# The low part of w2's rows on GpSimd in the one-block dense layers of a linear-attention kernel

## The chip, the cores and the metric

The kernel runs on one core of a Trainium2 chip. The metric is the device time of one execution in microseconds. TensorE (PE) multiplies matrices, VectorE (DVE), ScalarE (ACT) and GpSimd (POOL) work elementwise, and SyncE (SP) issues nearly all transfers. Each engine runs its own queue in order and waits on semaphores for the others.

## What is computed

Two rounds of a linear-attention layer A and a dense layer B on x of 2048 x 576, all in float32:

```python
def _A_ref(x, wqkv, w_phi, wo):          # H = 32 heads of 18
    q, k, v = heads(x @ wqkv)
    pq, pk = q @ w_phi, k @ w_phi         # per head
    phi_q = concat(softmax(pq), softmax(-pq))
    phi_k = concat(softmax(pk), softmax(-pk))
    kv, z = phi_k.T @ v, phi_k.sum(over s)
    return (phi_q @ kv / (phi_q @ z + 1e-6)) @ wo

def _B_ref(x, w1, b1, w2, b2):           # 576 -> 4608 -> 576
    h = relu(x @ w1 + b1)
    return (h * h) @ w2 + b2

x = A_x
for _ in range(2):
    x = x + _A_ref(layernorm(x), A_wqkv, A_w_phi, A_wo)
    x = x + _B_ref(layernorm(x), B_w1, B_b1, B_w2, B_b2)
```

## The kernel before

The 2048 rows are four blocks of 512. A matrix product in float32 is made of three products of parts: each operand is split into a high part, which ScalarE writes in the type fp32r that TensorE multiplies, and a low part, the operand less its high part, which VectorE or GpSimd subtracts. High x high, high x low and low x high are summed.

Each round has, behind a barrier at which the sums over all keys are complete, a dense layer for each block. Two blocks are done one by one with `g_mlp` (a first pass and a second pass), the other two together with `g_pair`. In the trace the first pass of the first round is `m_3`, the second pass `m_2`, and in the second round `m_1` and `m_0`; they lie at about 219 to 498, 490 to 808, 1426 to 1705 and 1694 to 2017 us, and both rounds run nearly alike. Beside the first pass runs the attention of the next block (`back_first`), beside the second pass that of the last two (`back_second`): tiles named `a_0`, `a_1`, `a_2`, `a_3`. The function `weave` interleaves the two by a rate, and `chained` keeps the steps of the attention in their order on VectorE, ScalarE and GpSimd. The final order of each engine's queue is set when the program is built, by a planner with costs and due times, so it can differ from the order in which the lines are traced; `tc.issue_after` fixes one instruction behind another.

A pass goes over 36 groups f of 128 hidden features. For each group:

- `first(f)` loads w1's columns into r1 (L1159, L244) and w2's rows into r2 (L1161). ScalarE makes the high parts: L1167 of w1, L1168 of the 448 columns of w2 that `by_rows` uses, L1169 of the 128 that `features` uses. The low part of w1 is L1171. `low()` makes the two low parts of w2: L1174 for the rows (128x448, VectorE), L1175 for the features (128x128, GpSimd).
- `hidden(f)` is 14 matmuls on x (L1190), `square(f)` applies bias, Relu and Square on ScalarE (L1197 to L1199) and makes the low part of the result on VectorE (L1200).
- `second(f - 1)` is 12 matmuls by rows (L1217) and 3 for the features (L1208). The high part of w2 enters in the first matmul of L1217, the low part in the second.

r1, r2, h1 and s2 have two buffers each, so r2 is loaded for a group when both low parts of the group two before are done.

For the first pass of a round `g_mlp` is called with `rest`, the unfinished end of the attention behind the keys. Then the first two groups are `early`: L1171 is on GpSimd for them, and `low()` is called later, behind given instructions. In all other groups `early` is false.

The attention that runs beside has its own work on the same queues: VectorE and GpSimd share products and scalings (L652 and L653, L835, L853), VectorE sums (L661, L841) and transposes the features (L897), SyncE stores them (L900) and loads them back turned (L928), ScalarE and VectorE split them (L941, L942), TensorE multiplies (L964, L999), and GpSimd adds b2 (L1051). At the end of the second pass the first operands of `g_pair` are prepared (L1478 to L1487 on GpSimd).

Of the kernel before, what the change touches and what calls it, by code (L numbers as in the profile page):

```python
# [7 lines left out]
F32 = mybir.dt.float32  # L8
# [13 lines left out]
def layers_kernel(  # L22
# [18 lines left out]
    nc = tc.nc  # L41
# [26 lines left out]
    RO = 16  # L68
# [25 lines left out]
    def wtile(name):  # L94
        n = len(spare["tags"])
        spare["i"] += 1
        i = spare["i"] % (n + 2)
        if i < n:
            return ps_a.tile([P, TB], F32, tag=spare["tags"][i], name=name)
        return ps_w.tile([P, TB], F32, tag="w", name=name)  # L100
# [140 lines left out]
    def load_twice(dst, src, c0, n):  # L241

        for i in range(2):
            nc.sync.dma_start(dst[i * DT : (i + 1) * DT], src[KC * P :, c0 : c0 + n])  # L244
# [902 lines left out]
    def g_mlp(layer, b, x, after, name, rest=None, then=None):  # L1147
# [3 lines left out]
        R = D - P  # L1151
# [3 lines left out]
        def first(f, early=False):  # L1155
            cols = slice(f * P, (f + 1) * P)
            r1 = sb.tile([P, NC, P], F32, tag="r1", name=f"{name}r1_{f}")
            r2 = sb.tile([P, D], F32, tag="r2", name=f"{name}r2_{f}")
            nc.sync.dma_start(r1[:, :KC], w1[: KC * P, cols].rearrange("(c p) n -> p c n", p=P))  # L1159
            load_twice(r1[:, KC], w1, f * P, P)  # L1160
            nc.sync.dma_start(r2, w2[cols])  # L1161
            hl1 = sb.tile([P, NC * HP], F32R, tag="h1", name=f"{name}h1_{f}")
            h1 = hl1[:, : NC * P].rearrange("p (c n) -> p c n", n=P)
            l1 = hl1[:, NC * P : 2 * NC * P].rearrange("p (c n) -> p c n", n=P)
            s2 = sb.tile([P, NC * HP], F32R, tag="s2", name=f"{name}s2_{f}")
            with tc.issue_after(dense["turn", 2 * f + 1].ins) if early else nullcontext():
                nc.scalar.activation(h1, r1, AF.Copy)  # L1167
            nc.scalar.activation(s2[:, RO : RO + R], r2[:, :R], AF.Copy)  # L1168
            nc.scalar.activation(s2[:, FC : FC + P], r2[:, R:], AF.Copy)  # L1169
            with tc.issue_after(dense["scaled1"].ins) if early else nullcontext():  # L1170
                dense["lowered"] = (nc.gpsimd if early else nc.vector).tensor_sub(l1, r1, h1.bitcast(F32))  # L1171

            def low():
                nc.vector.tensor_sub(s2[:, RO + R : RO + 2 * R], r2[:, :R], s2[:, RO : RO + R].bitcast(F32))  # L1174
                nc.gpsimd.tensor_sub(s2[:, FC + P : FC + 2 * P], r2[:, R:], s2[:, FC : FC + P].bitcast(F32))  # L1175

            if early:
                lows.append(low)
            else:
                low()  # L1180
            ph = wtile(f"{name}ph{f}") if f == 1 else ps_a.tile([P, TB], F32, tag="h", name=f"{name}ph{f}")
            parts[f] = (h1, l1, s2, ph)
# [650 lines left out]
    for layer in range(2):  # L1833
        ready, raws = barrier(layer, b, prev, x, xprev, kes, vpair, qpair)
        spare["tags"] = []
        early, operands, rows, nxt, keep = [], {}, [], {}, {}
# [148 lines left out]
```

## Time and profile before

| | |
|---|---|
| median of 3 runs | 2440.04 us (2438.57 to 2442.45) |
| the profiled execution | 2441.59 us |
| its span, first to last instruction | 2439.9 us |
| mean granted TensorE clock | 0.998 |
| PE busy | 2410.0 us (99%) |
| DVE busy | 1560.5 us (64%) |
| ACT busy | 1289.7 us (53%) |
| POOL busy | 940.6 us (39%) |

The columns of a row of the trace in order of time: start in us, duration in us, engine, line of the kernel, operation, output tile <- input tiles, shapes, count, and in brackets how long the engine sat idle before and what ended that. Rows of like instructions in a stretch are merged, with their count. In the view by groups stand the busy time and the mean in ns, and then the idle time before the group with what ended it. In the view of waits stand the waiting line, what it waited for, the total in us, how often, and the longest. In the view by stage each engine's busy time stands with its number of instructions, and then the granted clock and the transfers. A queue of an engine's sequencer has a q behind its name (SPq).

### The profile page before, as it was taken

What the parts mean: (1) busy time and instruction counts of PE and PEld (TensorE: products, weight loads), DVE (VectorE), ACT (ScalarE), POOL (GpSimd) and SP (SyncE); (2) the same over time, 40 slices, a digit from 0 to 9 for tenths busy, and PEclk for the clock granted to TensorE, in tenths of its full rate; (3) what the DMA queues carried; (4) which work ended last, traced back from release to release, by engine and by line L of the source; (5) the groups of instructions that cost most, each with busy time, mean ns of one, the idle gap of its engine ahead of it and who ended that gap; (6) DMA issues with size and microseconds to landing.
All of it is one profiled execution on the core that took longest, in us unless ns stands there. A gap on an engine that the chain in (4) does not pass through costs nothing. (4 is left out here: it accounts for less than half of the span.)

```text
span 2439.9 us, 41475 instructions
## 1 busy us (share of the span) xinstructions
PE 2410.0 (99%) x14806; PEld 2137.9 (88%) x14806; DVE 1560.5 (64%) x2537; ACT 1289.7 (53%) x2543; POOL 940.6 (39%) x1121
## 2 busy tenths in 40 slices
PE   9999999999999999999999999999999999999999
PEld 8999888888888888888999988888887888888898
DVE  8779847664867655545766787486557675555443
ACT  4344555444456666664443444554455466676643
POOL 4555303212335565542433442032222455565321
PEclk9999999999999999999999999999999999999999
DMA  9124573666654533338753156537667444333364
GB/s 338 64 84 165 163 194 97 151 202 220 155 173 136 157 99 115 109 104 302 257 188 139 59 173 143 168 96 186 191 233 158 141 142 145 118 103 116 110 199 130
DMA packets 370646, 379.40 MB, mean 155 GB/s; under 512 B 142886, under 2 KB 270790, under 8 KB 367878
## 3 DMA queue, kind: packets, MB, share of 16 engines
q1 hardware_dynamic: 369180, 375.37, 51.2%
q8 instruction: 116, 1.90, 0.3%
q10 hardware_dynamic: 1258, 1.37, 0.2%
q14 instruction: 92, 0.75, 0.1%
HBM read 297.22 MB, written 79.41 MB: 154 GB/s over the span
## 5 line engine op out<-in xcount | busy, mean ns | idle before, releaser
L1507 POOL TENSOR_TENSOR m_ps<-m_pr,m_ps 128x128 fp32r<-128x128 f32 x144 | 98.6, 685 | 337.8 <-ACT m_ps L1505 310.7
L1506 DVE TENSOR_TENSOR m_ps<-m_pr,m_ps 128x448 fp32r<-128x448 f32 x144 | 99.8, 693 | 175.9 <-ACT m_ps L1504 175.8
L1549 PE MATMUL m_pacc<-m_ps,m_phb 128*128 128x448 f32 x864 | 185.6, 363 | 0.0
L1549 PEld LDWEIGHTS m_pacc<-m_ps,m_phb 128*128 128x128 f32 x864 | 161.9, 188 | 15.0
L1549 PE MATMUL m_pacacc<-m_ps,m_phc 128*128 128x448 f32 x648 | 147.1, 365 | 0.0
L1504 ACT ACTIVATE m_ps<-m_pr 128x448 fp32r<-128x448 f32 x144 | 82.8, 575 | 115.7 <-issue 64.9
L1549 PEld LDWEIGHTS m_pacacc<-m_ps,m_phc 128*128 128x128 f32 x648 | 119.2, 188 | 7.7
L1190 PE MATMUL m_0ph<-a_0nh,m_0h 128*128 128x512 f32 (+1 forms) x380 | 96.7, 382 | 1.6 <-ACT m_0hr L1197 1.4
L1190 PE MATMUL m_1ph<-t1onh,m_1h 128*128 128x512 f32 (+1 forms) x380 | 96.2, 381 | 2.0 <-ACT m_1hr L1197 1.8
L1217 PE MATMUL m_2acc<-m_2s,m_2hb 128*128 128x448 f32 x432 | 95.2, 367 | 2.9 <-ACT m_2s L1168 2.6
L1190 PE MATMUL m_3ph<-t0onh,m_3h 128*128 128x512 f32 (+1 forms) x380 | 96.1, 381 | 1.8 <-ACT m_3hr L1197 1.6
L1217 PE MATMUL m_0acc<-m_0s,m_0hb 128*128 128x448 f32 x432 | 95.0, 367 | 2.9 <-ACT m_0s L1168 2.6
L1190 PE MATMUL m_2ph<-a_2nh,m_2h 128*128 128x512 f32 (+1 forms) x380 | 96.6, 382 | 0.8 <-ACT m_2hr L1197 0.6
L1217 PE MATMUL m_3acc<-m_3s,m_3hb 128*128 128x448 f32 x432 | 94.2, 364 | 2.0 <-ACT m_3hb L1198 1.4
L1217 PE MATMUL m_1acc<-m_1s,m_1hb 128*128 128x448 f32 x432 | 94.2, 364 | 2.0 <-ACT m_1hb L1198 1.4
L1217 PEld LDWEIGHTS m_2acc<-m_2s,m_2hb 128*128 128x128 f32 x432 | 81.8, 190 | 11.7 <-ACT m_2s L1168 3.0
L1217 PEld LDWEIGHTS m_0acc<-m_0s,m_0hb 128*128 128x128 f32 x432 | 81.5, 190 | 11.7 <-ACT m_0s L1168 3.0
L1217 PEld LDWEIGHTS m_3acc<-m_3s,m_3hb 128*128 128x128 f32 x432 | 80.4, 188 | 10.6 <-ACT m_3hb L1198 2.1
L1217 PEld LDWEIGHTS m_1acc<-m_1s,m_1hb 128*128 128x128 f32 x432 | 80.4, 188 | 10.5 <-ACT m_1hb L1198 2.1
L1175 POOL TENSOR_TENSOR m_3s<-m_3r,m_3s 128x128 fp32r<-128x128 f32 x36 | 22.9, 637 | 161.9 <-ACT m_3s L1169 153.3
L1175 POOL TENSOR_TENSOR m_1s<-m_1r,m_1s 128x128 fp32r<-128x128 f32 x36 | 22.8, 635 | 162.0 <-ACT m_1s L1169 151.8
L1190 PEld LDWEIGHTS m_1ph<-t1onh,m_1h 128*128 128x128 f32 x380 | 68.8, 188 | 17.4 <-ACT m_1hr L1197 3.0
(2464 smaller groups left out, 7237.0 us busy)
## 6 DMA issues: line engine op xcount, KB each, us to landing
m_pr<-in_B_w SPq DMA_DIRECT2D x144, 288.0 KB
m_pr<-in_B_w SPq DMA_DIRECT2D x72, 256.0 KB
hd<-m_pu SPq DMA_DIRECT2D x72, 256.0 KB
m_pg<-hd SPq DMA_DIRECT2D x72, 256.0 KB
m_3r<-in_B_w SPq DMA_DIRECT2D x36, 288.0 KB
m_2r<-in_B_w SPq DMA_DIRECT2D x36, 288.0 KB
m_1r<-in_B_w SPq DMA_DIRECT2D x36, 288.0 KB
m_0r<-in_B_w SPq DMA_DIRECT2D x36, 288.0 KB
```

Source lines behind the costliest of these rows:

```text
L1175: nc.gpsimd.tensor_sub(s2[:, FC + P : FC + 2 * P], r2[:, R:], s2[:, FC : FC + P].bitcast(F32))
L1190: dense["hidden"] = nc.tensor.matmul(ph[:, cols], a, m, start=(k == 0), stop=(k == len(ops) - 1))
L1217: nc.tensor.matmul(acc[t][:, :R], a[:, rows], m, start=(f == 0 and k == 0), stop=(f == NF - 1 and k == 2))
L1504: nc.scalar.activation(s2[:, RO : RO + R], r2[:, :R], AF.Copy)
L1506: nc.vector.tensor_sub(s2[:, RO + R : RO + 2 * R], r2[:, :R], s2[:, RO : RO + R].bitcast(F32))
L1507: nc.gpsimd.tensor_sub(s2[:, FC + P : FC + 2 * P], r2[:, R:], s2[:, FC : FC + P].bitcast(F32))
L1549: nc.tensor.matmul(accs[b][t][:, :R], a[:, rows], m, start=(g == 0 and k == 0), stop=(g == NF - 1 and k == 2))
```

## The change

In `low()` the subtraction of L1174 goes to GpSimd, unless the group is `early`. The early groups are the first two of the first pass of each round. L1175 stays on GpSimd in all groups, behind the moved instruction in the order of the lines.

```diff
             def low():
-                nc.vector.tensor_sub(s2[:, RO + R : RO + 2 * R], r2[:, :R], s2[:, RO : RO + R].bitcast(F32))
+                (nc.vector if early else nc.gpsimd).tensor_sub(s2[:, RO + R : RO + 2 * R], r2[:, :R], s2[:, RO : RO + R].bitcast(F32))
                 nc.gpsimd.tensor_sub(s2[:, FC + P : FC + 2 * P], r2[:, R:], s2[:, FC : FC + P].bitcast(F32))
```

## The prediction

> **What bounds the kernel now.** I read the page's engine line, then the busy time by stage, then what TensorE waited for, then the moved line and the stretches around those waits in order of time.
>
> ```profile
> span 2439.9 us, 41475 instructions
> ## 1 busy us (share of the span) xinstructions
> PE 2410.0 (99%) x14806; PEld 2137.9 (88%) x14806; DVE 1560.5 (64%) x2537; ACT 1289.7 (53%) x2543; POOL 940.6 (39%) x1121
> ```
> ```profile
> core 0: us, PE busy (x) PEld busy (x) DVE busy (x) ACT busy (x) POOL busy (x), PEclk, DMA share, GB/s
> ...
> 270.00:490.00 220.00, 216.27 (x1061) 187.85 (x1060) 142.05 (x210) 112.05 (x207) 49.26 (x53) 1.00 0.56 140
> ...
> 1750.00:2002.00 252.00, 246.66 (x1264) 216.54 (x1263) 163.25 (x267) 129.04 (x254) 90.59 (x111) 0.99 0.58 169
> ```
>
> TensorE is the bound, in the dense stages too: 216.27 of 220 us and 246.66 of 252. Neither VectorE (142 and 163) nor GpSimd (49 and 91) is full over a stage, so the change can move the end only through waits of TensorE. Those are few. The views of the waits, for a first dense pass (270 to 490) and for the second passes (1711 to 2002, 540 to 795), name them:
>
> ```profile
> PE m_3acc L1217 <- ACT m_3hb L1198: 1.4, 1, 1.4
> PE m_3acc L1217 <- DVE m_3s L1174: 0.6, 1, 0.6
> ```
> ```profile
> PE m_0acc L1217 <- ACT m_0s L1168: 2.6, 1, 2.6
> PE m_0ph L1190 <- ACT m_0hr L1197: 1.4, 1, 1.4
> PE a_2pn L964 <- ACT a_2fh L941: 1.1, 1, 1.1
> PE m_0acc L1217 <- DVE m_0s L1174: 0.3, 1, 0.3
> ```
> ```profile
> PE m_2ph L1190 <- ACT m_2hr L1197: 0.6, 1, 0.6
> PE a_1pn L964 <- ACT a_1fh L941: 0.4, 1, 0.4
> ```
>
> The moved line, L1174, is named in two of them, 0.6 and 0.3 us. The rest is behind ScalarE, and so behind transfers and the attention chain that runs beside.
>
> **The change part by part.**
>
> *Removed from VectorE.* In each of the four dense passes the low part of w2's rows (128x448) goes to GpSimd in place of VectorE; the two early groups of each first pass stay. That is 4 x 36 - 4 = 140 instructions.
>
> ```profile
> L1174 DVE TENSOR_TENSOR m_3s<-m_3r,m_3s 128x448 fp32r<-128x448 f32 x36 | 26.9, 751 | 3.1 <-ACT m_3s L1168 3.0
> ```
>
> 140 x 0.75 us is at most 105 us less VectorE, none of it on TensorE's path by itself.
>
> *Added to GpSimd.* No row has a subtraction of 128x448 there. The nearest on either side:
>
> ```profile
> L1478 POOL TENSOR_TENSOR m_ps<-m_pr,m_pr 128x384 f32<-128x384 f32 x36 | 36.7, 1020 | 2.2
> ...
> L1051 POOL TENSOR_TENSOR a_3x<-a_3x,b2t 128x576 f32<-128x576 f32 x4 | 5.7, 1433 | 3.8 <-DVE a_3ne L1292 2.9 <-PE m_0ph L1190 0.9
> ```
>
> Bounds 1.02 and 1.43 us; by the width between, 1020 + 64/192 x 413 = 1158 ns. I take 1.2 us, since neighbours stretch such rows. 140 x 1.2 = 168 us; GpSimd goes from 940.6 to about 1109 us, 45% of the span, and cannot become the bound of a stage (90.6 + 36 x 1.2 = 134 of 252). The Trainium skill (GPSIMD Engine Reference, section 4.1 Engine selection) advises VectorE for plain two-input arithmetic, GpSimd being about twice as slow. The rows agree on the price, 1.2 against 0.7; taken as a rule for the time, with every loss on the path, the sum would be 140 x 0.45 = 63 us slower. By the rows it is nothing, since TensorE hardly waits for L1174.
>
> *What is queued behind it.* On GpSimd the new instruction stands just ahead of L1175 of its group, so L1175 ends up to 1.2 us later. L1175's result is used three matmul groups after the rows' low part, and no wait of TensorE on L1175 is listed: zero. The rows' low part itself is first used by the second matmul of `second`. Of the groups in steady flow the tightest is:
>
> ```profile
> 295.42 0.56 ACT L1168 ACTIVATE m_3s<-m_3r 128x448 fp32r<-128x448 f32 x1
> ...
> 297.45 0.58 DVE L1174 TENSOR_TENSOR m_3s<-m_3r,m_3s 128x448 fp32r<-128x448 f32 x1
> ...
> 299.59 0.77 PE L1217 MATMUL m_3acc<-m_3s,m_3hb 128*128 128x448 f32 x3
> ```
>
> GpSimd could start at 295.98 and end at 297.2; TensorE comes at 299.6, so 2.4 us are left, where VectorE, which had it in its queue, left 1.6. The same cover hides the release of w2's buffer, on which SyncE's next w2 load waits: now VectorE's end (298.03), then L1175's, about 297.2 + 0.46. No DMA is moved to another queue. This cover hides the longer instruction. If it were gone, each such group would cost up to 1.2 us.
>
> *The group where TensorE waits for L1174 in the first passes (0.6 us).*
>
> ```profile
> 456.66 0.46 POOL L1175 TENSOR_TENSOR m_3s<-m_3r,m_3s 128x128 fp32r<-128x128 f32 x1
> ...
> 457.33 0.61 DVE L1174 TENSOR_TENSOR m_3s<-m_3r,m_3s 128x448 fp32r<-128x448 f32 x1
> ...
> 457.99 1.27 PE L1217 MATMUL m_3acc<-m_3s,m_3hb 128*128 128x448 f32 x5 [0.56 <-DVE m_3s L1174]
> ```
>
> The new one would start where L1175 starts, 456.66, and end at 457.9, as VectorE does now (457.94). The wait stays: 0, between -0.6 (GpSimd takes it in an earlier gap) and +0.7 (it falls behind L1175's 0.46 and stretches).
>
> *The group of the long wait in the second passes.*
>
> ```profile
> 1856.35 2.30 SPq L900 DMA_DIRECT2D a_2ft<-a_2Q1e  x4
> ...
> 1858.75 0.62 SPq L1161 DMA_DIRECT2D m_0r<-in_B_w  x1
> ...
> 1863.86 0.69 ACT L1197 ACTIVATE m_0hr<-m_0ph,b1t 128x512 f32<-128x512 f32 x1 [4.26 <-PE m_0ph L1190]
> ...
> 1865.78 0.56 ACT L1168 ACTIVATE m_0s<-m_0r 128x448 fp32r<-128x448 f32 x1
> ...
> 1866.39 0.47 PE L1217 MATMUL m_0acc<-m_0s,m_0hb 128*128 128x448 f32 x1 [2.57 <-ACT m_0s L1168]
> 1866.52 0.62 DVE L1174 TENSOR_TENSOR m_0s<-m_0r,m_0s 128x448 fp32r<-128x448 f32 x1
> ...
> 1867.19 3.72 PE L1217 MATMUL m_0acc<-m_0s,m_0hb 128*128 128x448 f32 x11 [0.32 <-DVE m_0s L1174]
> ```
>
> Here w2 comes late: its load stands on SyncE behind the turned features' stores (L900), and ScalarE's split stands behind L1197 to L1199 in ScalarE's order. TensorE needs the low part at once. VectorE gives it at 1867.14; GpSimd would at about 1866.37 + 1.2 = 1867.6: +0.43 us, in both layers +0.9.
>
> *VectorE relieved, and what that releases.* Ahead of that wait VectorE is full, and five of the moved instructions stand there:
>
> ```profile
> 1822.00:1856.00 34.00, 34.00 (x158) 29.33 (x157) 33.79 (x48) 18.48 (x33) 14.49 (x13) 1.00 0.39 100
> ```
> ```profile
> L1174 DVE TENSOR_TENSOR m_0s<-m_0r,m_0s x5: 579/608/614, 1824.1 to 1853.4; 128x448 fp32r<-128x448 f32 x5
> ```
>
> VectorE works 33.79 of 34 us, GpSimd 14.49. Each removed L1174 lets the attention chain's VectorE work, and the stores L900 behind it, come up to 0.61 us sooner: at most 5 x 0.61 = 3 us. Against it stands that the two engines get in each other's way:
>
> ```profile
> 1833.01 1.69 POOL L853 TENSOR_TENSOR a_2Q0e<-a_2Q0e,a_2Q0r 128x576 f32<-128x576 f32 x1
> ...
> 1833.59 1.72 DVE L853 TENSOR_TENSOR a_2Q0e<-a_2Q0e,a_2Q0r 128x576 f32<-128x576 f32 x1
> ...
> 1846.54 0.74 DVE L853 TENSOR_TENSOR a_2Q1e<-a_2Q1e,a_2Q1r 128x576 f32<-128x576 f32 x1
> ```
>
> Alone VectorE's L853 takes 0.74 us; beside a GpSimd instruction it takes 1.72 and ends 0.6 us behind that one, as if it had waited it out. So a moved instruction gives 0.61 us back and can take up to 1.2: between +0.6 and -0.6 us each, +3 and -3 us over five. I take +0.5 us for the chain, near the middle, since about half of VectorE's work there reads one SBUF tensor or PSUM. Half a microsecond sooner shortens the four waits behind the chain in the second passes (1.4, 1.1, 0.6, 0.4) by 0.5, 0.5, 0.5 and 0.4: -1.9 us, between -3.5 and +3.5.
>
> **The sum.** Against the profiled execution (2441.59 us, its span 2439.9 and 1.7 around it): +0.9 - 1.9 = -1.0, so 2440.6. The median of the runs, 2440.04, lies 1.55 under that execution, and the same step from it gives 2439.0.
>
> **The rivals.**
>
> *A new order takes the long wait away (faster).* The order on each engine is a planner's, from costs and due times, not the program's. With VectorE's queue shorter in its count, the w2 load or ScalarE's split of that group can be put ahead of L1197, in the 4.26 us in which ScalarE stands idle. Then the wait of 2.57 and 0.32 goes, and the slow matmuls behind it, 3.72 us for 11 against 2.36 for the same 11 elsewhere:
>
> ```profile
> 299.79 2.36 PE L1217 MATMUL m_3acc<-m_3s,m_3hb 128*128 128x448 f32 x11
> ```
>
> 2.57 + 0.32 + 1.36 = 4.25 us a layer, 8.5 for both: 2440.04 - 8.5 - 1.9 = 2429.6. For it speaks the full VectorE ahead of that place; against it that the idle 4.26 us were not used now, and that nothing in the trace shows the planner's own times. The waits of the first passes (1.4) could go likewise.
>
> *GpSimd holds VectorE (slower).* If the moved instruction, as L853 above, makes VectorE wait it out, the chain loses 0.6 us for each of five instead of gaining. The stores L900 and the w2 load behind them come 3 us later, in that same place: the 2.57 us wait becomes 5.6, with another 1.4 us of slow matmuls behind it: 4.4 a layer. 2440.04 + 0.9 + 2 x 4.4 = 2449.7. It decides from the point where an instruction costs VectorE more than 0.61 us. For it speaks the 1.72 against 0.74; against it that L1174 already runs beside L1175 now (751 ns in the mean, 608 in the five above), and that GpSimd is idle 19.5 of the 34 us. The Trainium skill (GPSIMD Engine Reference, section 1 Specifications) says that GpSimd's SBUF interfaces are shared with VectorE and contended by instructions of two SBUF inputs; by that rule this is what happens, and the trace agrees with the rule in the 1.72 us, though not on how often it would strike.
>
> *Nothing moves at all:* no wait changes but the 0.43: 2440.9, inside the forecast's own range.
>
> **How the numbers follow.** Within 0.2% (4.9 us), about what a measurement here can tell, is the forecast's own range, 2435.2 to 2444.9: 0.42, the most likely. Faster: 0.33, the new order. Slower: 0.25, GpSimd holding VectorE, or a new order that is worse. The terms of the forecast all stay under 4 us, and only a doubled stall, once in each layer, leaves that band. The range reaches to both rivals: 2428 to 2450.
>
> **What would show it.** Right: L1174 on POOL x140 at 1.1 to 1.4 us; VectorE's total down by 60 to 100 us; the 2.57 us wait still there, with some 0.7 us behind POOL L1174 after it; waits on L941 and L1197 in the second passes shorter. Wrong toward faster: TensorE no longer waits for L1168. Wrong toward slower: L853, L835 and L1171 on VectorE longer in the mean, the stores L900 later, and the wait for L1168 longer. What would make the prediction wrong is another order of TensorE's groups in either pass, since each layer repeats it.

## The result: 0.6% slower, at a few places

The changed kernel takes 2453.8 us (median of 4 runs, 2452.89 to 2455.38) beside 2440.26 us of the kernel before on the same chip: 1.0056, interval 1.0038 to 1.0073, or +13.5 us. Of the profiled execution the head of the page reads:

```profile
span 2451.1 us, 41229 instructions
## 1 busy us (share of the span) xinstructions
PE 2412.6 (98%) x14806; PEld 2136.1 (87%) x14806; DVE 1493.7 (61%) x2397; ACT 1289.3 (53%) x2543; POOL 1090.1 (44%) x1261
```

VectorE's busy time fell by 66.8 us, GpSimd's rose by 149.5, and the span grew by 11.2 us: 2.6 us of busy TensorE, the rest TensorE waiting. The moved line by tile, minimum, median and maximum in ns, and when it ran:

```profile
L1174 POOL TENSOR_TENSOR m_2s<-m_2r,m_2s x36: 1139/1158/1677, 501.2 to 799.2; 128x448 fp32r<-128x448 f32 x36
...
L1174 POOL TENSOR_TENSOR m_3s<-m_3r,m_3s x34: 1134/1161/1710, 241.8 to 488.6; 128x448 fp32r<-128x448 f32 x34
```

**Where the time went.** The order of ScalarE's queue is the same in both kernels and TensorE's differs in a few neighbouring matmuls, so the two traces (one execution of each) can be set side by side by the start of the first L1217 of each `second(f)`. How much later that start is in the changed kernel, and by how much this grows at each place (first round, second round):

| place | growth, us |
|---|---|
| first passes, group 2 | 1.4, 1.1 |
| first passes, all other groups | 0.8, 0.7 |
| second passes, groups 0 and 1 | 1.2, 1.2 |
| second passes, groups 8 and 9 | 1.3, 0.9 |
| second passes, groups 17 to 20 | -1.0, -1.4 |
| second passes, group 26 | 0.4, 0.3 |
| second passes, groups 33 and 34 | 2.0, 1.5 |
| the last pair | 1.1 |

The sum is 11.5 us, against 11.2 of the span (the changed kernel's first pass began 0.3 us sooner). Between these places hardly anything grows. Not all rows are equally firm. Group 2, groups 0 and 1 and groups 33 and 34 stay within 0.5 us of the kernel before in every run below that leaves them as they were. Groups 17 to 20 do not: in e1_first, whose second passes are not changed, they differ by +1.7 and -1.0 us.

At these places stand new or longer waits of TensorE. Waits of the changed kernel in the stretches 219 to 270, 500 to 545 and 545 to 800 us (total, times, longest):

```profile
PE m_3ph L1190 <- ACT m_3hr L1197: 1.1, 1, 1.1
```
```profile
PE m_2ph L1190 <- DVE a_2nl L521: 0.9, 1, 0.9
```
```profile
PE a_1qp L606 <- DMA a_1uh<-xth: 1.6, 1, 1.6
PE m_2ph L1190 <- ACT m_2hr L1197: 1.2, 1, 1.2
PE m_2acc L1217 <- POOL m_2s L1174: 0.8, 1, 0.8
```

In the kernel before, the first is absent, the second is 0.2 us, and the third is 0.3. Only the last one names the moved line. The others are two steps away from it, by three ways.

The clearest is group 2 of the first pass; in order of time, before and then after:

```profile
242.09 0.70 POOL L1175 TENSOR_TENSOR m_3s<-m_3r,m_3s 128x128 fp32r<-128x128 f32 x1 [4.54 <-ACT m_3s L1169]
242.76 1.17 POOL L653 TENSOR_TENSOR a_2Q0e<-a_2Q0m,t0q2qs 128x576 f32<-128x576 f32 x1
...
243.96 1.17 ACT L657 ACTIVATE a_2Q0e<-a_2Q0e 128x1152 f32<-128x1152 f32 x1 [1.94 <-POOL a_2Q0e L653]
245.03 0.67 ACT L1197 ACTIVATE m_3hr<-m_3ph,b1t 128x512 f32<-128x512 f32 x1
...
246.11 1.31 PE L1190 MATMUL m_3ph<-t0onh,m_3h 128*128 128x512 f32 x5
```
```profile
241.75 1.46 POOL L1174 TENSOR_TENSOR m_3s<-m_3r,m_3s 128x448 fp32r<-128x448 f32 x1 [4.48 <-ACT m_3s L1168]
243.17 0.45 POOL L1175 TENSOR_TENSOR m_3s<-m_3r,m_3s 128x128 fp32r<-128x128 f32 x1
243.59 1.68 POOL L653 TENSOR_TENSOR a_2Q0e<-a_2Q0m,t0q2qs 128x576 f32<-128x576 f32 x1
...
245.31 1.17 ACT L657 ACTIVATE a_2Q0e<-a_2Q0e 128x1152 f32<-128x1152 f32 x1 [3.44 <-POOL a_2Q0e L653]
246.38 0.67 ACT L1197 ACTIVATE m_3hr<-m_3ph,b1t 128x512 f32<-128x512 f32 x1
...
247.10 1.43 PE L1190 MATMUL m_3ph<-t0onh,m_3h 128*128 128x512 f32 x5 [1.15 <-ACT m_3hr L1197]
```

Behind L1174 and L1175 on GpSimd stands the attention's subtraction L653. ScalarE's exponential L657 waits for it, ScalarE's order puts the dense layer's Relu L1197 behind L657, and the next hidden matmuls of TensorE need L1197. No wait for the moved instruction's own result is listed there.

At groups 0 and 1 of the second pass GpSimd's queue is not the way. Beside the moved instruction VectorE itself is slower: its scaling L490 takes 1.36 us in place of 0.81 (rows in the last section), the L495 behind it 0.48 in place of 0.33. VectorE's subtraction L521, further back in the same queue, comes 0.7 us later, and TensorE waits 0.9 us for it in place of 0.2. A little later VectorE's L942 takes 1.22 us beside the moved instruction of group 2 where it took 0.68, and TensorE waits 0.3 us for it.

At groups 8 and 9 of the second pass the w2 load on SyncE comes later, before and then after:

```profile
574.74 0.58 ACT L1168 ACTIVATE m_2s<-m_2r 128x448 fp32r<-128x448 f32 x1 [0.65 <-PE m_2acc L1208]
...
576.32 0.35 SPq L1161 DMA_DIRECT2D m_2r<-in_B_w  x1
...
577.71 1.18 SPq L1346 DMA_DIRECT2D ptt<-a_0nt  x1
584.27 0.32 SPq L593 DMA_DIRECT2D a_1uh<-xth  x1
```
```profile
577.93 0.58 ACT L1168 ACTIVATE m_2s<-m_2r 128x448 fp32r<-128x448 f32 x1 [0.66 <-PE m_2acc L1208]
...
579.70 0.47 POOL L1175 TENSOR_TENSOR m_2s<-m_2r,m_2s 128x128 fp32r<-128x128 f32 x1
...
580.19 0.35 SPq L1161 DMA_DIRECT2D m_2r<-in_B_w  x1
...
583.18 1.05 SPq L1346 DMA_DIRECT2D ptt<-a_0nt  x1
586.29 0.33 SPq L593 DMA_DIRECT2D a_1uh<-xth  x1
...
595.42 0.91 PE L606 MATMUL a_1qp<-a_1q0h,a_1uh 128*128 128x288 f32 x5 [1.60 <-DMA a_1uh<-xth]
```

The w2 load L1161 waits for the buffer that L1175 releases. From ScalarE's split it now takes 2.26 us in place of 1.58, and the last store of the normalised rows queued behind it on SyncE comes 5.25 us after the split in place of 2.97. The attention's matmul L606, which needs the load L593 behind them, is the 1.6 us wait above. This way is not shown to its end: L593 itself is issued no later after the split (8.36 us in place of 9.53) and lands later after its issue, and in e2_second, which moves the same instructions, this place costs -0.3 us in the first round and 1.1 in the second.

At group 33 the preparation of the last pair stands behind the moved instruction (L1478 to L1487 on GpSimd), and ScalarE's L1472 waits for it with L1197 behind, before and then after:

```profile
782.36 0.53 ACT L1472 ACTIVATE m_pwa<-m_pr 128x384 fp32r<-128x384 f32 x1 [3.33 <-POOL m_pr L1487]
...
785.38 1.31 PE L1190 MATMUL m_2ph<-a_2nh,m_2h 128*128 128x512 f32 x5
```
```profile
781.28 1.16 POOL L1174 TENSOR_TENSOR m_2s<-m_2r,m_2s 128x448 fp32r<-128x448 f32 x1
...
787.21 1.02 POOL L1487 TENSOR_TENSOR m_pr<-m_pr,m_ps 128x384 f32<-128x384 f32 x1
788.26 0.53 ACT L1472 ACTIVATE m_pwa<-m_pr 128x384 fp32r<-128x384 f32 x1 [5.28 <-POOL m_pr L1487]
...
789.99 0.67 ACT L1197 ACTIVATE m_2hr<-m_2ph,b1t 128x512 f32<-128x512 f32 x1
790.70 1.42 PE L1190 MATMUL m_2ph<-a_2nh,m_2h 128*128 128x512 f32 x5 [1.22 <-ACT m_2hr L1197]
```

Group 26 goes the same way on a small scale, by ScalarE's L1419, which waits 2.78 us for GpSimd's L1405 in place of 1.21.

### The profile page after: what moved, and what is told of

The parts are those of the page before. It is cut to its first block, busy times and chain, and to the rows that moved or that the text cites. A ratio compares the mean times of both kernels' runs of the same rounds, so it can differ in the third digit from the quotient of the medians.

```text
span 2451.1 us, 41229 instructions
## 1 busy us (share of the span) xinstructions
PE 2412.6 (98%) x14806; PEld 2136.1 (87%) x14806; DVE 1493.7 (61%) x2397; ACT 1289.3 (53%) x2543; POOL 1090.1 (44%) x1261
## 5 line engine op out<-in xcount | busy, mean ns | idle before, releaser
L1174 POOL TENSOR_TENSOR m_3s<-m_3r,m_3s 128x448 fp32r<-128x448 f32 x34 | 42.0, 1236 | 137.5 <-ACT m_3s L1168 120.9
L1174 POOL TENSOR_TENSOR m_1s<-m_1r,m_1s 128x448 fp32r<-128x448 f32 x34 | 41.7, 1227 | 137.8 <-ACT m_1s L1168 122.4
L1190 PE MATMUL m_2ph<-a_2nh,m_2h 128*128 128x512 f32 (+1 forms) x380 | 97.2, 383 | 2.4 <-ACT m_2hr L1197 1.2
L1217 PE MATMUL m_0acc<-m_0s,m_0hb 128*128 128x448 f32 x432 | 94.9, 367 | 3.3 <-ACT m_0s L1168 2.6
L1217 PE MATMUL m_2acc<-m_2s,m_2hb 128*128 128x448 f32 x432 | 93.8, 364 | 3.3 <-ACT m_2s L1168 2.6
L1217 PE MATMUL m_3acc<-m_3s,m_3hb 128*128 128x448 f32 x432 | 94.2, 364 | 2.3 <-ACT m_3hb L1198 1.4
L1217 PE MATMUL m_1acc<-m_1s,m_1hb 128*128 128x448 f32 x432 | 94.2, 364 | 2.3 <-ACT m_1hb L1198 1.4
L1217 PEld LDWEIGHTS m_0acc<-m_0s,m_0hb 128*128 128x128 f32 x432 | 81.5, 190 | 12.1 <-ACT m_0s L1168 3.0
L1174 POOL TENSOR_TENSOR m_0s<-m_0r,m_0s 128x448 fp32r<-128x448 f32 x36 | 42.7, 1186 | 109.0 <-ACT m_0s L1168 103.6
L1217 PEld LDWEIGHTS m_2acc<-m_2s,m_2hb 128*128 128x128 f32 x432 | 80.7, 188 | 11.9 <-ACT m_2s L1168 3.0
L1174 POOL TENSOR_TENSOR m_2s<-m_2r,m_2s 128x448 fp32r<-128x448 f32 x36 | 43.3, 1201 | 107.4 <-ACT m_2s L1168 101.8
L1217 PEld LDWEIGHTS m_3acc<-m_3s,m_3hb 128*128 128x128 f32 x432 | 80.4, 188 | 10.8 <-ACT m_3hb L1198 2.1
```

What stands on the lines that cost most here:

```text
L1174: (nc.vector if early else nc.gpsimd).tensor_sub(s2[:, RO + R : RO + 2 * R], r2[:, :R], s2[:, RO : RO + R].bitcast(F32))
L1190: dense["hidden"] = nc.tensor.matmul(ph[:, cols], a, m, start=(k == 0), stop=(k == len(ops) - 1))
L1217: nc.tensor.matmul(acc[t][:, :R], a[:, rows], m, start=(f == 0 and k == 0), stop=(f == NF - 1 and k == 2))
```

## The experiments

Two theories. **Q, the queue:** the moved instruction stands ahead of other work of GpSimd, at a few places another engine waits for that work, and fixed orders carry the delay to TensorE. **H, the hold:** beside the longer GpSimd work VectorE is slower wherever both run, and that is what TensorE feels. The runs test H as a cost spread over all 140 instructions; groups 0 and 1 above show that it can also act at one place. Every difference below is a median against the median of the kernel before on the same chip.

**e1_first and e2_second: one kind of pass each.**

```diff
-(nc.vector if early else nc.gpsimd).tensor_sub(...)
+(nc.gpsimd if rest and f > 1 else nc.vector).tensor_sub(...)   # e1_first
+(nc.vector if rest else nc.gpsimd).tensor_sub(...)             # e2_second
```

> L1174 goes to GpSimd only in the first passes (68 instructions); the second passes are as before. Theory Q (queue): the loss lies in a few places where the moved 1.16 us stand on GpSimd ahead of an instruction of the neighbouring work that ScalarE waits for in its fixed order, with L1197 and so TensorE behind it. In the traces TensorE lost 1.9 us in m_3 and 1.7 in m_1, so Q expects 3 to 5 us more than before, and the wait for L1197 at the third group (1.1 us) there. Theory H (held): the loss is VectorE waiting out GpSimd's instructions all along, so it goes by count and by how full VectorE is, and the first passes have 68 of the 140 with VectorE at 46 of 51 us in their first stretch: 6.5 to 9 us more.

> L1174 goes to GpSimd only in the second passes (72 instructions). Q: TensorE lost 4.0 us in m_2 and 2.5 in m_0 in the trace of the change, and a last 1.1 us in the pair behind: 6 to 9 us more than before. H: by count, 5 to 7 us more. The two runs together should give the 13.5 us of the change if the losses add.

Measured: e1_first 2445.65, +4.4 us (1.0017, 1.0008 to 1.0026); e2_second 2448.53, +7.3 (1.0032, 1.0021 to 1.0044). Both medians lie in Q's ranges and outside H's, the second only just. Together they make 11.7 of 13.5, equal within the intervals (1.9 to 6.3 and 5.1 to 10.7).

**e3_spared: 20 instructions at and just ahead of the places stay on VectorE, 120 of 140 are moved.** Group 26, which costs 0.4 us, is not among the 20.

```diff
+(nc.vector if f in ((0, 1, 2, 30) if rest else (0, 1, 2, 8, 17, 31, 32, 33)) else nc.gpsimd).tensor_sub(...)
```

> L1174 goes to GpSimd as in the change, but for the groups ahead of the places where TensorE newly waited: groups 2 and 30 of the first passes, 0, 1, 2, 8, 17, 31, 32 and 33 of the second. 120 of the 140 stay moved. Q: the new waits go with those 20 groups, and the time comes back to within 3 us of before. H: 120 of 140 of the loss stay, 10 to 12 us more than before.

Measured: 2439.65, -1.6 us (0.9994, 0.9985 to 1.0003): the same as before, with six sevenths of the change in place. So the 20 instructions cost all of it, 14 to 15 us (2453.8 less 2439.65, or by the differences to before); H, spread over the instructions, falls. The order of VectorE's and ScalarE's other instructions is the same as in the changed kernel, so a new order on these two engines is not the cause either.

**e12_ten: the reverse, 10 instructions moved.**

```diff
+(nc.gpsimd if not rest and f in (0, 1, 31, 32, 33) else nc.vector).tensor_sub(...)
```

> L1174 is on GpSimd only in groups 0, 1, 31, 32 and 33 of the second passes: 10 instructions in place of 140, VectorE relieved of the same 10. Theory Q (queue): these places cost what they show in the changed kernel's trace, +1.2 us a layer at groups 0 and 1 and +1.5 to +2.0 at groups 31 to 33, so +5.5 to +6.5 us in all against before. Theory H (VectorE held wherever both run, by the instruction): 10/140 of the change's 13.5 us, some +1 us, at most +2.

Measured: 2446.25, +5.1 us (1.0021, 1.0012 to 1.0030): ten instructions of 1.16 us, 11.6 us of work on an engine that is idle for over half of the span, cost 5.1. By its trace groups 0 and 1 cost 0.7 us in each round (VectorE held, as above) and groups 33 and 34 cost 1.9 and 1.5 (GpSimd's queue).

**e7_behind and e8_one: group 2 of the first passes.** e7_behind leaves all 140 on GpSimd and only queues L1174 and L1175 of that group behind the attention's two L653 (the orders of the other three engines stay those of the changed kernel); e8_one keeps L1174 of that group on VectorE.

```diff
+with tc.issue_after(dense["parted", 1].ins) if rest and f == 2 else nullcontext(): ...   # e7_behind: both low parts
+(nc.vector if early or rest and f == 2 else nc.gpsimd).tensor_sub(...)                   # e8_one
```

> The change, but in group 2 of the first passes both low parts of w2 (L1174 and L1175, still on GpSimd) are queued behind the attention's two L653 in place of ahead of them. The queues of TensorE, ScalarE and VectorE are the same as in the change. Q: L653 and the exponential behind it (L657) come as early as before, so L1197 is not held and the wait of 1.1 us (m_3) and 1.3 us (m_1) for it at that group goes: 2 to 3 us faster than the change, 10 to 12 slower than before. H: the same number of instructions on GpSimd with the same VectorE beside them, no gain: 13 to 14 us slower than before.

> The change, but group 2 of the first passes keeps L1174 on VectorE: 2 of the 140 instructions. Q: the same 2 to 3 us as in the run that queues it behind L653, 10 to 12 us slower than before. H: 2 of 140 are worth 0.2 us.

Measured: 2449.83, +8.0 us (1.0032, 1.0020 to 1.0043), and 2450.0, +8.2 (1.0034, 1.0021 to 1.0047), against +13.5 (9.3 to 17.8 by its interval). The wait is gone in both, and the same GpSimd work in another order does as well as none. In e7_behind, in order of time:

```profile
241.93 1.61 POOL L653 TENSOR_TENSOR a_2Q0e<-a_2Q0m,t0q2qs 128x576 f32<-128x576 f32 x1 [4.35 <-DVE a_2Q0m L649]
243.58 1.17 ACT L657 ACTIVATE a_2Q0e<-a_2Q0e 128x1152 f32<-128x1152 f32 x1 [1.57 <-POOL a_2Q0e L653]
...
244.65 0.67 ACT L1197 ACTIVATE m_3hr<-m_3ph,b1t 128x512 f32<-128x512 f32 x1
245.49 1.15 POOL L1174 TENSOR_TENSOR m_3s<-m_3r,m_3s 128x448 fp32r<-128x448 f32 x1
246.14 1.30 PE L1190 MATMUL m_3ph<-t0onh,m_3h 128*128 128x512 f32 x5
```

This is the direct test of Q, for this place. The firm part is the wait that is gone. The gain of some 5 us is more than the 2.4 that the waits at that place account for, and its size is not settled: the intervals touch (4.9 to 10.5 against 9.3 to 17.8).

**e6_half: 224 columns on each engine.**

```diff
+for a, e in ((0, nc.vector if early else nc.gpsimd), (R // 2, nc.vector)): e.tensor_sub(s2[:, RO + R + a : ...], ...)
```

> GpSimd takes 224 of the 448 columns, VectorE the other 224, in the same 140 groups. GpSimd's part should take some 0.7 us in place of 1.16. Q: the same places, each with the wait that 0.7 us leave: where the attention had no slack the wait falls by 0.46, so 4 to 8 us slower than before. H: VectorE has two instructions in place of one and still waits: 8 to 14 us.

Measured: 2449.68, +7.9 us (1.0032, 1.0019 to 1.0044): half the work ahead of the neighbour, a little over half the loss. It does not part the theories: Q's range ended at 8 and H's began there.

**e5_extra and e11_apart: GpSimd loaded, VectorE not relieved.** L1174 stays on VectorE; GpSimd does two subtractions of 128x224 into unused columns of s2, in all 140 groups (e5_extra) or in the 120 of e3_spared alone (e11_apart).

```diff
+nc.vector.tensor_sub(...); early or [nc.gpsimd.tensor_sub(s2[:, FC + 2 * P : ...], r2[:, i : ...], ...) for i in (0, R // 2)]
```

> L1174 stays on VectorE in all groups, and GpSimd does beside it, in the same 140 groups and at the same place of its queue, two subtractions of 128x224 of the same operands into unused columns of s2. GpSimd has a little more to do than in the change, VectorE is not relieved. Q: the same places wait, by about 1.3 us in place of 1.16: 12 to 18 us more than before, and about as slow as the change, since the relief of VectorE bought nothing. H: VectorE has its own 140 and waits for GpSimd besides: 18 to 30 us more. If the relief was worth the 2 us that the prediction gave it, this is slower than the change by at least that.

> L1174 stays on VectorE, and GpSimd does the two extra subtractions of 128x224 into unused columns only in the 120 groups that e3_spared left moved; the 20 groups at stage borders have none. Theory Q (queue): the extra work costs only where ScalarE, SyncE or TensorE waits for what GpSimd does next; between -2 and +3 us against before. Theory H (VectorE held by GpSimd wherever both run): what e5_extra lost is spread over its 140 groups, so 120 of them lose about 120/140 of its 25.9 us, some +22 us, at least +15.

Measured: e5_extra 2467.14, +25.9 us (1.0112, 1.0099 to 1.0126), more than Q allowed and within H's range; e11_apart 2453.61, +12.8 (1.0052, 1.0039 to 1.0065), between the two expectations, so both missed. The difference, 13.1, is what the 20 instructions cost here, near the 14 to 15 of the change. The other 12.8 has two sources. VectorE is busy for 1588.4 us, 27.9 more than before with the same instructions in the same order: that is the hold. But at group 26, which is not among the 20, TensorE waits for GpSimd's queue again, in both rounds; in the first:

```profile
746.25 0.42 ACT L1419 ACTIVATE a_1nt4h<-a_1nu 128x256 fp32r<-128x256 f32 x1 [3.03 <-POOL a_1nu L1405]
...
747.88 1.42 PE L1190 MATMUL m_2ph<-a_2nh,m_2h 128*128 128x512 f32 x5 [1.03 <-ACT m_2hr L1197]
```

By the trace this place costs 1.3 us in each round. How the remaining 10 us are shared was not separated. A new wait of TensorE for VectorE stands there too:

```profile
PE a_2po L999 <- DVE a_2nl L521: 1.1, 1, 1.1
```

It is weak evidence, since 0.4 us of it also stand in e4_left, where GpSimd does nothing more.

So the hold is real. It is there in the change as well: the removed instructions had been busy for 97.2 us and VectorE's busy time fell by only 66.8, and in e3_spared it is 84.4 against 50.1. There the relief of VectorE pays for it: 120 groups cost nothing that can be told (-1.6 us) with the relief and 12.8 without it. One caution: the two extra instructions take 1.73 us a group (207 us over 120), the moved one 1.16, so e11_apart also delays GpSimd's own queue more than the change does.

**e4_left: L1174 left out.** In the 140 groups the low part of w2's rows is not made, and TensorE multiplies by the high part again in its place.

```diff
+if early: nc.vector.tensor_sub(...)
...
-a, m = ((hh, hi), (hh, lo), (hl, hi))[k]
+a, m = ((hh, hi), (hh, lo if rest and f < 2 else hi), (hl, hi))[k]
```

> L1174 is left out in the 140 groups: neither engine makes the low part, and TensorE multiplies the high part a second time in its place, so its work is the same. This prices the relief of VectorE alone. Q: VectorE was not on TensorE's path in any place but those where TensorE waited for L1174 (0.6 and 0.3 us): 0 to 3 us faster than before. If the relief was worth what the prediction allowed at most, 3.5 us more than that: 4 to 6 us faster.

Measured: 2434.67, -7.1 us (0.9969, 0.9959 to 0.9979), more than Q's 3. Here the planner puts ScalarE's split L1168 ahead of the Relu at the place of the long wait, and the 2.6 us wait for L1168 is gone. That is the order of the prediction's first rival, so the next two made it by hand.

**e10_order and e9_ahead: that order alone.** e10_order is the kernel before, e9_ahead is e3_spared, each with

```diff
-nc.scalar.activation(s2[:, RO : RO + R], r2[:, :R], AF.Copy)
+dense["half", f] = nc.scalar.activation(s2[:, RO : RO + R], r2[:, :R], AF.Copy)
...
+with tc.issue_after(dense["half", 17].ins) if not rest and f == 18 else nullcontext(): nc.scalar.activation(hr, ph, ...)
```

> The kernel before (all of L1174 on VectorE) with one change of order: in the second passes ScalarE's split of w2's rows of group 17 (L1168, L1169) stands ahead of the Relu of group 18 (L1197). If the prediction's price for the long wait is right, TensorE's waits of 2.57 and 0.32 us and the 1.36 us of slow matmuls behind them go in both layers: -8.5 us against before, between -5 and -8.5. Rival: what is behind it only waits for the next late piece (the turned features of the attention, or the w2 load of group 18): between 0 and -2 us.

> e3_spared (120 of the 140 moved to GpSimd) with the same order on ScalarE for group 17 as e10_order. If the wait goes as in e10_order, both steps add: about -9 us against before (-0.6 of e3_spared and up to -8.5), at least as fast as e10_order within 1 us. Rival: the next late piece decides, as in e10_order, 0 to -2 us. If the relief of VectorE is worth something once that wait is gone, e9_ahead beats e10_order by 1 us or more.

Measured: e10_order 2441.5, +0.7 us (1.0002, 0.9992 to 1.0011); e9_ahead 2440.51, -0.3 (0.9997, 0.9988 to 1.0006). Nothing, in both. TensorE's waits in e10_order at that place (1855 to 1885 us):

```profile
PE m_0ph L1190 <- ACT m_0hr L1197: 1.5, 1, 1.5
PE m_0ph L1190 <- ACT m_0h L1167: 1.5, 1, 1.5
PE m_0acc L1217 <- DVE m_0s L1174: 1.5, 2, 1.3
```

and two of its rows:

```profile
1862.92 0.58 ACT L1168 ACTIVATE m_0s<-m_0r 128x448 fp32r<-128x448 f32 x1 [2.39 <-DMA m_0r<-in_B_w]
...
1874.17 0.74 ACT L1167 ACTIVATE m_0h<-m_0r 128x640 fp32r<-128x640 f32 x1 [4.40 <-DMA m_0r<-in_B_w]
```

The split comes 2.9 us earlier and TensorE is 2.7 us ahead (at the same start of `second`, 0.9 to -1.8). Two groups later it is at +0.5: w1 of the next groups lands no sooner, because its load stands behind the attention's stores and loads on SyncE, and ScalarE waits 4.40 us for it. The wait moved on to the next late transfer. Why e4_left keeps part of its gain there (2.3 and 3.8 us over those groups) while these two do not was not separated; its VectorE is relieved without any added GpSimd work. No version that does the whole computation beat the kernel before clear of the noise.

## Why the prediction was wrong, step by step

- **Removed from VectorE: right.** Its busy time fell by 66.8 us, inside the 60 to 100 named.
- **Added to GpSimd: right.** 1158 ns as the interpolation gave, 149.5 us in all beside 168.
- **The group of the long wait: right.** The 2.57 us stays, and 0.8 behind POOL L1174 follows it, as named; +0.5 against +0.43.
- **VectorE relieved: the sign came out as forecast in this trace, the size is not shown.** The store L900 of a_2Q1e starts at 1862.06 where it was 1856.35, with TensorE 9.7 us late by then: 4.0 us sooner than TensorE's work (predicted at most 3). The 1.4 us wait on L1197 behind it is gone. Groups 17 to 20 gain 1.0 and 1.4 us, the loss of the step above included; the sum of both steps was put at -1.0 for the two layers and is -2.4. But with the same second passes e7_behind has -2.5 there, e8_one -0.2 and e2_second about 0, and e1_first, with those of before, has +0.8: a single trace does not tell such an amount.
- **What is queued behind it on GpSimd: the step that failed.** The prediction looked at L1175 of the same group and at its reader on TensorE, found cover, and set zero. It did not ask what stands behind L1175 on GpSimd: L653 at group 2 and L1478 to L1487 at group 33, whose readers sit in ScalarE's queue ahead of the Relu. By trace these two places cost 2.5 and 3.5 us in the two rounds.
- **The hold of VectorE, counted in one stretch only: failed too.** The prediction allowed for it over five instructions ahead of the long wait. It cost 2.4 us by trace at groups 0 and 1 of the second passes, where L490, L495 and L942 are stretched and TensorE is near. Its +0.5 us for the chain leaned on VectorE's work that reads one SBUF tensor; L490 reads one and is stretched.
- **"The same cover hides the release of w2's buffer": failed** at groups 8 and 9, by trace 2.2 us in both layers, with the open end named above. The group taken as the tightest, at 295 us, was the tightest for L1217, not for SyncE.
- **All of these together** cost 14 to 15 us (the changed kernel against e3_spared), from 20 of 140 instructions, where the sum had nothing.
- **First-pass group with the 0.6 us wait: right, within its bounds.** Put at zero between -0.6 and +0.7; the wait (270 to 490 us) is 0.3 longer:

```profile
PE m_3acc L1217 <- POOL m_3s L1174: 0.9, 1, 0.9
```

- **The rival "GpSimd holds VectorE"** named 2449.7, near the time measured, by another way: its long wait did not grow. The hold it rests on exists (e11_apart), but away from groups 0 and 1 the relief pays for it in the change (e3_spared). The rule of the Trainium skill that it cited (GPSIMD Engine Reference, section 1 Specifications: GpSimd's SBUF interfaces are shared with VectorE) agrees with VectorE's 27.9 us in e11_apart.
- **The rival "a new order takes the long wait away"** was priced at 4.25 us a layer. e10_order shows the price was wrong too: the wait went, and a later transfer took the gain back.
- **"Only a doubled stall, once in each layer, leaves that band":** several small ones in each layer did.

## What to carry to other kernels

A moved instruction is priced by what stands behind it in its new queue, and by what stands behind the readers of that, two steps on, at each border between stages; not by its own reader in the steady state. Twenty of 140 instructions decided here. The trace before showed the clearest places: ScalarE sat idle 1.94 us for GpSimd's L653 and 3.33 us for its L1487. So follow the new engine's next instructions to an engine that sits idle for them, and look also at which of VectorE's instructions will run beside the moved one where TensorE is about to need them. In this kernel the largest wait, taken away by reordering, gave its time back two groups later at the next late transfer.

## What was not expected of the hardware

VectorE is stretched by a GpSimd subtraction also when its own instruction reads one SBUF tensor (and two columns of scalars): the normalisation's scaling L490 with no GpSimd subtraction beside it and beside L1175 (both before), then beside the moved instruction (after):

```profile
494.14 0.55 DVE L490 TENSOR_SCALAR a_2nn<-a_2x,a_2nm,a_2nd 128x512 f32<-128x512 f32 x1 [0.54 <-POOL a_2nd L464]
...
499.32 0.81 DVE L490 TENSOR_SCALAR a_2nn<-a_2x,a_2nm,a_2nd 128x512 f32<-128x512 f32 x1 [0.44 <-POOL a_2nd L464]
499.39 0.46 POOL L1175 TENSOR_TENSOR m_2s<-m_2r,m_2s 128x128 fp32r<-128x128 f32 x1
```
```profile
501.18 1.14 POOL L1174 TENSOR_TENSOR m_2s<-m_2r,m_2s 128x448 fp32r<-128x448 f32 x1
501.25 1.36 DVE L490 TENSOR_SCALAR a_2nn<-a_2x,a_2nm,a_2nd 128x512 f32<-128x512 f32 x1 [0.43 <-POOL a_2nd L464]
```

It took 0.55 us alone, 0.81 beside the 0.46 us of L1175, and 1.36 beside the 1.14 us of the moved instruction, ending 0.29 us behind it. The trace before had it already: at 45.98 us, beside GpSimd's L653, a scaling of the same shape takes 1.39 us.
